# An MLP half rewritten: GELU in one ScalarE instruction, 64-row matmul pairs for a short K-chunk, bias taken off TensorE

## The chip, the cores and the metric

The kernel runs on one core of a Trainium2 chip. The metric is the device time of one execution, in microseconds (us). Engines are called PE (TensorE matmul), PEld (TensorE weight load, which overlaps PE), DVE (VectorE), ACT (ScalarE), POOL (GpSimd) and SP (SyncE, which only issues transfers here). The profile's span is a little shorter than the time (607.4 against 609.1 us for the kernel before). A ratio below is the mean time of one kernel's fast runs over that of the other's fast runs of the same rounds, so it is not quite the ratio of the medians that are quoted beside it.

## The reference

One transformer layer: layer norm, a linear-attention mixer, a residual add, two more layer norms, an MLP with GELU, and a second residual add. 2048 tokens, width 576, hidden width 4608, bf16. The change lies in the MLP:

```python
def _B_ref(x, w1, b1, w2, b2):
    y = _layernorm(x, axis=-1)
    h = _gelu(jnp.einsum("bsd,df->bsf", y, w1) + b1)     # tanh form
    return jnp.einsum("bsf,fd->bsd", h, w2) + b2

h  = x + _A_ref(_layernorm(x), ...)                      # attention part
h2 = h + _B_ref(_layernorm(h), B_w1, B_b1, B_w2, B_b2)   # MLP part
```

576 is not a multiple of 128: the contraction over it falls into four chunks of 128 rows and one of 64.

## The kernel before

The MLP works on blocks of 512 tokens (four in all). FF1 makes hidden features in m-tiles of 128 (36 of them), FF2 contracts them again. Before that a stage called LN2 here normalizes all 16 token tiles and transposes them into `ln2T`. The fifth K-chunk is padded with zero rows (cuts marked `# ...`):

```python
ln2T = []
for c in range(NKC):                       # KC = [128, 128, 128, 128, 64]
    t = persist.tile([P, S], BF16, ...)
    if KC[c] < P:
        nc.gpsimd.memset(t[:, :], 0.0)     # padding, done in the set-up
# ... attention part ...
w1c[4]: nc.gpsimd.memset(t, 0.0), then a DMA of 64 rows
w2t: first half on the SP queue, second half on the POOL queue
# LN2: per pair of token tiles: tensor_scalar on DVE, transposes (128 x 128, the last one
# 128 x 64), PSUM to SBUF on ACT (chunks 0, 2, 4) and DVE (chunks 1, 3)
for b in range(NBK):
    for half in range(2):                                    # 18 m-tiles each
        h1T = hpool.tile([P, NHALF, 512], BF16, ...)         # one buffer
        for pair in range(NHALF // 2):
            for i in range(2):                               # FF1: 5 matmuls of 128x512
                # ...
                nc.scalar.activation(x1[:, i, :], ph, AF.Identity, bias=b1col[:, m : m + 1])
            nc.vector.tensor_tensor(ga, x1, x1, ALU.mult)    # GELU by hand
            nc.vector.tensor_scalar(gb, ga, GELU_A, 1.0, ALU.mult, ALU.add)
            nc.vector.tensor_tensor(gc, gb, x1, ALU.mult)
            nc.scalar.activation(gs, gc, AF.Sigmoid, scale=GELU_C2)
            nc.vector.tensor_tensor(h1T[:, mm0 : mm0 + 2, :], x1, gs, ALU.mult)
        for j in range(4):                                   # FF2: 18 x (512 + 64 columns)
            if half == 0:                                    # b2 as two one-row matmuls
                nc.tensor.matmul(po1[:, 0:512], ones_row, b2row[:, 0:512], start=True, stop=False)
                nc.tensor.matmul(po2[:, 0:64], ones_row, b2row[:, 512:D], start=True, stop=False)
            # ... matmuls over mm, then h_all[:, t] += po1, po2 on DVE
    # ... ot = copy(h_all) on ACT, DMA out
```

The softmax here doesn't subtract the row's maximum and nothing guards it: scores larger than these inputs give would overflow.

## Time and profile before

The time is 609.06 us (median of 4 runs). The attention part ends at about 268 us; the MLP takes the rest.

| Part of the MLP, in a steady block of 512 tokens | us | Read from |
|---|---|---|
| FF1, 180 matmuls of 128x512, one every 0.216 us | 38.9 | timeline |
| FF2, 144 pairs of 512 + 64 columns, one every 0.245 us | 35.3 | timeline |
| b2, 4 pairs of one-row matmuls, 0.47 us each | 1.9 | timeline |
| rest: mostly PE waiting at FF1-to-FF2 borders | 3.4 | 79.53 minus the above |
| one block | 79.53 | first FF1 matmul of a block to that of the next |

These groups of instructions are from the page of the kernel before. The columns are: line, engine, operation, output from inputs and shapes, count; busy us and mean ns of one; idle us just before them and what ended most of it.

```profile
L579 PE MATMUL ph<-ln2T,w1c 128*128 128x512 bf16 x720 | 157.6, 380 | 0.0
L615 PE MATMUL po<-w2t,h1T 128*128 128x512 bf16 x576 | 146.8, 381 | 11.7 <-DVE h1T L598 11.4
L585 ACT ACTIVATE x<-ph,b1col 128x512 bf16<-128x512 f32 x144 | 91.9, 681 | 74.5 <-PE ph L579 74.5
L589 DVE TENSOR_TENSOR ga<-x 128x1024 bf16<-128x1024 bf16 x72 | 49.6, 689 | 22.3 <-ACT x L585 22.3
L597 ACT ACTIVATE gs<-gc 128x1024 bf16<-128x1024 bf16 x72 | 75.9, 1055 | 22.8 <-DVE gc L595 22.8
L598 DVE TENSOR_TENSOR h1T<-x,gs 128x1024 bf16<-128x1024 bf16 x72 | 49.5, 687 | 10.4 <-ACT gs L597 9.7
```

FF1 (L579) never waits. The first FF2 matmuls (L615) wait 11.4 us for `h1T`, the last step of the GELU chain. That chain costs DVE 0.69 + 0.43 + 0.69 + 0.69 = 2.5 us per pair of m-tiles, which overlap to 2.27 where DVE doesn't wait (timeline, 376.02 to 378.29 us) and to some 2.35 on average, while PE makes a pair in 10 x 0.216 = 2.16 us. So DVE falls behind through the half, and PE pays at the border. ACT has little slack either: where it doesn't wait, its two Identities and the Sigmoid take 2.09 us per pair (374.74 to 376.83).

The next lines are from the timeline around one pair of b2 matmuls: start and duration in us, then the instruction. The durations overlap (0.39 us for 512 columns that start every 0.216 us) and the ends are modelled, so starts are to be compared.

```profile
399.22 0.19 PE L621 MATMUL po<-w2t,h1T 128*128 128x64 bf16 x1
399.34 0.39 PE L606 MATMUL po<-b2row,ones_row 1*128 1x512 bf16 x1
399.57 0.19 PE L609 MATMUL po<-b2row,ones_row 1*128 1x64 bf16 x1
399.69 0.39 PE L615 MATMUL po<-w2t,h1T 128*128 128x512 bf16 x1
```

From 399.22 to 399.69 is 0.47 us, of which the ordinary 64-column matmul's own slot is 0.03. At each change between 128 rows and 1 row some 0.09 us is lost: 399.34 - 399.22 is 0.12 where an ordinary 64-column matmul takes 0.03.

### The profile page before, as it was taken

To read this page: it belongs to the slowest core of one execution; us is meant where nothing else is said; L and a number is where in the kernel's file an instruction comes from. 1 tells how busy PE (TensorE), PEld (TensorE's weight loads), DVE (VectorE), ACT (ScalarE), POOL (GpSimd) and SP (SyncE) were. 2 spreads that over 40 slices of the span, in tenths; PEclk is the share of its full clock that TensorE was granted. 3 is DMA by queue.
4 is the path that set the end of the run, shared out by engine and by line. 5 is a ranking of instruction groups with operands and counts; after the bars stand their busy time and mean duration, and the time that the engine had idled before them with its cause. 6 is when DMAs were issued, how large, how long until landed. Compare 5 with 4: busy or idle time off the path is not lost.

```text
span 607.4 us, 9204 instructions
## 1 busy us (share of the span) xinstructions
PE 506.7 (83%) x3626; PEld 268.9 (44%) x3626; DVE 396.6 (65%) x997; ACT 271.7 (45%) x470; POOL 35.5 (6%) x95
## 2 busy tenths in 40 slices
PE   0169777987878788759999999999899998999986
PEld 0136546773344544425444444444444444444443
DVE  3807998651588889985864928639468195492771
ACT  1155678525303030014944818429266084480661
POOL 8620000020000000030000000000000000000000
PEclk9999789797669697776999999999999999999999
DMA  8000000010000000049600000000000000000001
GB/s 288 2 0 3 1 0 2 2 29 16 1 2 1 1 1 1 2 165 326 210 2 1 0 30 11 0 1 1 21 19 1 1 1 11 30 0 2 1 1 39
DMA packets 10261, 18.61 MB, mean 31 GB/s; under 512 B 1513, under 2 KB 8490, under 8 KB 9642
## 3 DMA queue, kind: packets, MB, share of 16 engines
q1 hardware_dynamic: 9049, 15.36, 7.5%
q0 software_dynamic: 1168, 2.67, 1.4%
q8 instruction: 28, 0.46, 0.3%
q14 instruction: 16, 0.12, 0.1%
HBM read 15.66 MB, written 2.36 MB: 30 GB/s over the span
## 4 chain that ended last, share of the span: by engine, by line
DVE 44%; PE 41%; ACT 10%; issue 3%; DMA 2%; POOL 1%; ACTq 0%; DVEq 0%; POOLq 0%
PE po L615 15%; DVE h1T L598 7%; DVE gc L595 7%; PE ph L579 6%; DVE ga L589 6%; DVE gb L591 4%; ACT gs L597 3%; DVE sk L300 3%; DVE phik L309 3%; PE pbr L411 2%; ACT eq L386 2%; PE po L621 2%; PE pao L480 2%; PE pt L551 2%; PE pkA L285 2%
## 5 line engine op out<-in xcount | busy, mean ns | idle before, releaser
L579 PE MATMUL ph<-ln2T,w1c 128*128 128x512 bf16 x720 | 157.6, 380 | 0.0
L615 PE MATMUL po<-w2t,h1T 128*128 128x512 bf16 x576 | 146.8, 381 | 11.7 <-DVE h1T L598 11.4
L585 ACT ACTIVATE x<-ph,b1col 128x512 bf16<-128x512 f32 x144 | 91.9, 681 | 74.5 <-PE ph L579 74.5
L621 PE MATMUL po<-w2t,h1T 128*128 128x64 bf16 x576 | 109.5, 193 | 0.0
L579 PEld LDWEIGHTS <-w1c 128*128 128x128 bf16 x720 | 69.6, 98 | 84.5 <-DMA w1c<-in_B_w_dram 0.5
L615 PEld LDWEIGHTS <-h1T 128*128 128x128 bf16 x576 | 56.3, 98 | 84.1 <-DVE h1T L598 17.0
L597 ACT ACTIVATE gs<-gc 128x1024 bf16<-128x1024 bf16 x72 | 75.9, 1055 | 22.8 <-DVE gc L595 22.8
L627 DVE TENSOR_TENSOR h_all<-h_all,po 128x512 f32<-128x512 f32 x32 | 22.0, 689 | 89.2 <-PE po L621 89.2
L589 DVE TENSOR_TENSOR ga<-x 128x1024 bf16<-128x1024 bf16 x72 | 49.6, 689 | 22.3 <-ACT x L585 22.3
L621 PEld LDWEIGHTS <-h1T 128*128 128x128 bf16 x576 | 56.1, 98 | 1.5
L598 DVE TENSOR_TENSOR h1T<-x,gs 128x1024 bf16<-128x1024 bf16 x72 | 49.5, 687 | 10.4 <-ACT gs L597 9.7
L595 DVE TENSOR_TENSOR gc<-gb,x 128x1024 bf16<-128x1024 bf16 x72 | 49.6, 688 | 1.2
L386 ACT ACTIVATE eq<-ppq 128x512 bf16<-128x512 f32 x40 | 21.6, 595 | 60.4 <-PE ppq L377 60.4
L636 ACT CAST ot<-h_all 128x576 bf16<-128x576 f32 x16 | 10.7, 671 | 51.4 <-DVE h_all L630 51.4
L317 PE MATMUL pv<-wv,ln1T 128*128 128x504 bf16 x80 | 24.4, 423 | 10.7 <-DVE ln1T L275 6.6
L591 DVE TENSOR_SCALAR gb<-ga 128x1024 bf16<-128x1024 bf16 x72 | 30.8, 427 | 2.4
L402 DVE RECIPROCAL recrow<-psS 128x80 bf16<-128x80 f32 x16 | 10.5, 658 | 25.2 <-PE psS L394 25.0
L413 DVE TENSOR_TENSOR phiq<-eq,pbr 128x512 bf16<-128x512 bf16 x40 | 24.3, 681 | 3.0 <-PE pbr L411 3.0
L285 PEld LDWEIGHTS <-ln1T 128*128 128x128 bf16 x400 | 24.9, 104 | 0.8
L300 DVE TENSOR_REDUCE sk<-phik 128x64 f32<-128x1152 bf16 x16 | 21.2, 1331 | 5.9 <-ACT phik L296 5.8
L377 PE MATMUL ppq<-ln1T,Wq 128*128 128x512 bf16 x100 | 24.8, 410 | 0.0
L285 PE MATMUL pkA<-Wk,ln1T 128*128 128x128 bf16 x320 | 23.7, 232 | 0.0
(129 smaller groups left out, 592.8 us busy)
## 6 DMA issues: line engine op xcount, KB each, us to landing
w1c<-in_B_w_dram SPq DMA_DIRECT2D x4, 1152.0 KB
w2t<-in_B_w_dram POOLq DMA_DIRECT2D x1, 2592.0 KB, 23.1
w2t<-in_B_w_dram SPq DMA_DIRECT2D x1, 2592.0 KB
x_all<-in_A_x_dram SPq DMA_DIRECT2D x1, 2304.0 KB
out_dram<-ot SPq DMA_DIRECT2D x16, 144.0 KB
wqkv<-in_A_wqkv_dram SPq DMA_DIRECT2D x4, 432.0 KB
w1c<-in_B_w_dram SPq DMA_DIRECT2D x1, 576.0 KB
wog<-in_A_wo_dram SPq DMA_DIRECT2D x4, 141.8 KB
```

What stands on the lines that cost most here:

```text
L285: nc.tensor.matmul(dst, ln1T[c][:, t * 128 : (t + 1) * 128], wkp[(g, c)][:, :], start=(c == 0), stop=(c == NKC - 1),)
L300: nc.vector.tensor_reduce(sk[:, :], phik[:, t, :, :].rearrange("p s (h f) -> p (s h) f", f=DH), AX.X, ALU.add,)
L386: nc.scalar.activation(eq[:, :], ppq[:, :], AF.Exp, scale=sc)
L579: nc.tensor.matmul(ph[:, :], w1c[c][:, m * 128 : (m + 1) * 128], ln2T[c][:, b * 512 : (b + 1) * 512], start=(c == 0), stop=(c == NKC - 1),)
L585: nc.scalar.activation(x1[:, i, :], ph[:, :], AF.Identity, bias=b1col[:, m : m + 1], scale=1.0)
L589: nc.vector.tensor_tensor(ga[:, :, :], x1[:, :, :], x1[:, :, :], ALU.mult)
L591: nc.vector.tensor_scalar(gb[:, :, :], ga[:, :, :], GELU_A, 1.0, ALU.mult, ALU.add)
L595: nc.vector.tensor_tensor(gc[:, :, :], gb[:, :, :], x1[:, :, :], ALU.mult)
L597: nc.scalar.activation(gs[:, :, :], gc[:, :, :], AF.Sigmoid, scale=GELU_C2)
L598: nc.vector.tensor_tensor(h1T[:, mm0 : mm0 + 2, :], x1[:, :, :], gs[:, :, :], ALU.mult)
L615: nc.tensor.matmul(po1[:, 0:512], h1T[:, mm, j * 128 : (j + 1) * 128], w2t[:, m, 0:512], start=st_, stop=(mm == NHALF - 1),)
L621: nc.tensor.matmul(po2[:, 0 : D - 512], h1T[:, mm, j * 128 : (j + 1) * 128], w2t[:, m, 512:D], start=st_, stop=(mm == NHALF - 1),)
```

## The change

Its intent is to make PE the only limit of the MLP and to give it less to do. (1) GELU becomes one ACT instruction per m-tile. (2) b2 is broadcast once by DMA; POOL adds it to the residual ahead of time, and one DVE instruction makes the output tile. (3) The 64-row chunk is not padded: the weights of m-tile i sit on partitions 0 to 63, those of m-tile i+18 on 64 to 127, `ln2T[4]` holds its 64 rows twice, and the two 64-row matmuls stand side by side. They come last for even i and first for odd i, so two pairs meet. (4) FF1 runs over all 36 m-tiles before FF2; FF2 splits its columns 288 + 288. (5) All weights go through the SP queue; the paddings' memsets go. (6) PSUM: four banks for FF1 and LN2, two double-bank tiles for FF2.

```diff
-        if KC[c] < P:
-            nc.gpsimd.memset(t[:, :], 0.0)                   # ln2T padding
...
+        w1e = dpool.tile([P, NM // 2, P], BF16, name="w1e", tag="w1e")
+        for o in range(2):
+            nc.sync.dma_start(w1e[64 * o : 64 * o + 64, :, :], B_w1[512:D, o * FF // 2 : ...])
...
+                    nc.scalar.copy(ln2j[:, D : D + 64], ln2j[:, 512:D])   # rows twice
...
+                def rest(first):
+                    for o in range(2):
+                        r = slice(64 * o, 64 * o + 64)
+                        nc.tensor.matmul(phs[o], w1e[r, i, :], ln2T[4][r, tok], start=first, stop=not first)
+                odd = i % 2 == 1
+                if odd: rest(True)
+                for o in range(2): ...                       # 4 full matmuls each
+                if not odd: rest(False)
-                    ga, gb, gc, gs ... (DVE, DVE, DVE, ACT), h1T (DVE)
+                    nc.scalar.activation(h1T[:, m, :], phs[o], AF.Gelu_apprx_tanh, bias=b1col[:, m : m + 1])
...
-                        nc.tensor.matmul(po1[:, 0:512], ones_row[:, :], b2row[:, 0:512], ...)
-                        nc.tensor.matmul(po2[:, 0 : D - 512], ones_row[:, :], b2row[:, 512:D], ...)
+                nc.gpsimd.tensor_tensor(hb[:, :], h_all[:, t, :], b2bc[:, :], ALU.add)
+                nc.vector.tensor_tensor(ot, hb, pot[:, :, 0:288], ALU.add)
```

More of the change, by code (lines that the diff above doesn't have):

```diff
@@ L67 @@
     persist = ctx.enter_context(tc.tile_pool(name="persist", bufs=1))
-    psum = ctx.enter_context(tc.tile_pool(name="psum", bufs=6, space=bass.MemoryType.PSUM))
-    psum2 = ctx.enter_context(tc.tile_pool(name="psum2", bufs=1, space=bass.MemoryType.PSUM))
     actx = ctx.enter_context(ExitStack())
+    psum = actx.enter_context(tc.tile_pool(name="psum", bufs=6, space=bass.MemoryType.PSUM))
+    psum2 = actx.enter_context(tc.tile_pool(name="psum2", bufs=1, space=bass.MemoryType.PSUM))
     apool = actx.enter_context(tc.tile_pool(name="apool", bufs=1))
@@ L113 @@
     make_identity(nc, ident)
-    ones_row = consts.tile([1, P], BF16, name="ones_row", tag="ones_row")
-    nc.vector.memset(ones_row[:], 1.0)
     eps_ap = consts.tile([P, 1], FP32, name="eps_ap", tag="eps_ap")
     nc.vector.memset(eps_ap[:], EPS)
-    b2row = consts.tile([1, D], BF16, name="b2row", tag="b2row")
-    nc.sync.dma_start(b2row[:, :], B_b2.rearrange("(o f) -> o f", o=1))
+    b2bc = consts.tile([P, D], BF16, name="b2bc", tag="b2bc")
+    nc.sync.dma_start(b2bc[:, :], B_b2.rearrange("(o f) -> o f", o=1).to_broadcast([P, D]))
     b1nat = consts.tile([FF // P, P], BF16, name="b1nat", tag="b1nat")
@@ L520, with ln2_stage @@
         dpool = dctx.enter_context(tc.tile_pool(name="dpool", bufs=1))
+        pf = dctx.enter_context(tc.tile_pool(name="pf", bufs=4, space=bass.MemoryType.PSUM))
+        po = dctx.enter_context(tc.tile_pool(name="po", bufs=2, space=bass.MemoryType.PSUM))
+        NM = FF // P
         w1c = []
-        for c in range(NKC):
+        for c in range(4):
             t = dpool.tile([P, FF], BF16, name=f"w1c{c}", tag=f"w1c{c}")
-            if KC[c] < P:
-                nc.gpsimd.memset(t[:, :], 0.0)
-            nc.sync.dma_start(t[: KC[c], :], B_w1[KOFF[c] : KOFF[c] + KC[c], :])
+            nc.sync.dma_start(t[:, :], B_w1[KOFF[c] : KOFF[c] + P, :])
             w1c.append(t)
-        w2t = dpool.tile([P, FF // P, D], BF16, name="w2t", tag="w2t")
+        w1e = dpool.tile([P, NM // 2, P], BF16, name="w1e", tag="w1e")
+        for o in range(2):
+            nc.sync.dma_start(
+                w1e[64 * o : 64 * o + 64, :, :],
+                B_w1[512:D, o * FF // 2 : (o + 1) * FF // 2].rearrange("k (i p) -> k i p", p=P),
+            )
+        w2t = dpool.tile([P, NM, D], BF16, name="w2t", tag="w2t")
         w2v = B_w2.rearrange("(m p) f -> p m f", p=P)
         nc.sync.dma_start(w2t[:, 0:18, :], w2v[:, 0:18, :])
-        nc.gpsimd.dma_start(w2t[:, 18:36, :], w2v[:, 18:36, :])
+        nc.sync.dma_start(w2t[:, 18:36, :], w2v[:, 18:36, :])
         lnp2 = dctx.enter_context(tc.tile_pool(name="lnp2", bufs=4))
         small2 = dctx.enter_context(tc.tile_pool(name="small2", bufs=1))
+        hpool = dctx.enter_context(tc.tile_pool(name="hpool", bufs=1))
+        outp = dctx.enter_context(tc.tile_pool(name="outp", bufs=3))
+        hbp = dctx.enter_context(tc.tile_pool(name="hbp", bufs=2))
         rst2_all = small2.tile([P, NT], FP32, name="rst2_all", tag="rst2_all")
         nc.scalar.sqrt(rst2_all[:, :], ln2_r2[:, :])
-        for b in range(NBK):
+        def ln2_stage(b):
             for jp in range(2):
@@ L541 @@
                     t = 4 * b + j
-                    ln2j = lnp2.tile([P, D], BF16, name="ln2", tag="ln2")
+                    ln2j = lnp2.tile([P, D + 64], BF16, name="ln2", tag="ln2")
                     nc.vector.tensor_scalar(
-                        ln2j[:, :], h_all[:, t, :], ln2_mean[:, t : t + 1], rst2_all[:, t : t + 1],
+                        ln2j[:, 0:D], h_all[:, t, :], ln2_mean[:, t : t + 1], rst2_all[:, t : t + 1],
                         ALU.subtract, ALU.mult,
                     )
+                    nc.scalar.copy(ln2j[:, D : D + 64], ln2j[:, 512:D])
@@ L547 @@
                     ln2.append(ln2j)
+                tbase = (4 * b + 2 * jp) * 128
                 for c in range(NKC):
-                    pt = psum.tile([P, 256], BF16, name="pt2", tag="p1")
+                    pt = pf.tile([P, 256], BF16, name="pt2", tag="pf")
                     for jj in range(2):
                         nc.tensor.transpose(
-                            pt[: KC[c], jj * 128 : (jj + 1) * 128],
-                            ln2[jj][:, KOFF[c] : KOFF[c] + KC[c]],
-                            ident[:, :],
+                            pt[:, jj * 128 : (jj + 1) * 128], ln2[jj][:, c * P : (c + 1) * P], ident[:, :]
@@ L555 @@
                         )
-                    tbase = (4 * b + 2 * jp) * 128
                     if c % 2 == 0:
-                        nc.scalar.copy(ln2T[c][: KC[c], tbase : tbase + 256], pt[: KC[c], :])
+                        nc.scalar.copy(ln2T[c][:, tbase : tbase + 256], pt[:, :])
                     else:
-                        nc.vector.tensor_copy(ln2T[c][: KC[c], tbase : tbase + 256], pt[: KC[c], :])
-        hpool = dctx.enter_context(tc.tile_pool(name="hpool", bufs=1))
-        x1p = dctx.enter_context(tc.tile_pool(name="x1p", bufs=3))
@@ L566 @@
-        gpool = dctx.enter_context(tc.tile_pool(name="gpool", bufs=2))
-        outp = dctx.enter_context(tc.tile_pool(name="outp", bufs=2))
-        for b in range(NBK):
-            for half in range(2):
-                h1T = hpool.tile([P, NHALF, 512], BF16, name="h1T", tag="h1T")
-                for pair in range(NHALF // 2):
-                    mm0 = pair * 2
-                    x1 = x1p.tile([P, 2, 512], BF16, name="x1", tag="x1")
-                    for i in range(2):
-                        m = half * NHALF + mm0 + i
-                        ph = psum.tile([P, 512], FP32, name="ph", tag="p1")
-                        for c in range(NKC):
-                            nc.tensor.matmul(
-                                ph[:, :],
-                                w1c[c][:, m * 128 : (m + 1) * 128],
-                                ln2T[c][:, b * 512 : (b + 1) * 512],
-                                start=(c == 0), stop=(c == NKC - 1),
-                            )
-                        nc.scalar.activation(
-                            x1[:, i, :], ph[:, :], AF.Identity, bias=b1col[:, m : m + 1], scale=1.0
-                        )
-                    ga = gpool.tile([P, 2, 512], BF16, name="ga", tag="gab")
-                    nc.vector.tensor_tensor(ga[:, :, :], x1[:, :, :], x1[:, :, :], ALU.mult)
-                    gb = gpool.tile([P, 2, 512], BF16, name="gb", tag="gab")
-                    nc.vector.tensor_scalar(
-                        gb[:, :, :], ga[:, :, :], GELU_A, 1.0, ALU.mult, ALU.add
-                    )
-                    gc = gpool.tile([P, 2, 512], BF16, name="gc", tag="gc")
-                    nc.vector.tensor_tensor(gc[:, :, :], gb[:, :, :], x1[:, :, :], ALU.mult)
-                    gs = gpool.tile([P, 2, 512], BF16, name="gs", tag="gs")
-                    nc.scalar.activation(gs[:, :, :], gc[:, :, :], AF.Sigmoid, scale=GELU_C2)
-                    nc.vector.tensor_tensor(
-                        h1T[:, mm0 : mm0 + 2, :], x1[:, :, :], gs[:, :, :], ALU.mult
-                    )
-                for j in range(4):
-                    t = 4 * b + j
-                    po1 = psum.tile([P, 512], FP32, name="po1", tag="p1")
-                    po2 = psum.tile([P, 136], FP32, name="po2", tag="p1")
-                    if half == 0:
-                        nc.tensor.matmul(
-                            po1[:, 0:512], ones_row[:, :], b2row[:, 0:512], start=True, stop=False
-                        )
-                        nc.tensor.matmul(
-                            po2[:, 0 : D - 512], ones_row[:, :], b2row[:, 512:D], start=True, stop=False
-                        )
-                    for mm in range(NHALF):
-                        m = half * NHALF + mm
-                        st_ = (mm == 0) and (half == 1)
-                        nc.tensor.matmul(
-                            po1[:, 0:512],
-                            h1T[:, mm, j * 128 : (j + 1) * 128],
-                            w2t[:, m, 0:512],
-                            start=st_, stop=(mm == NHALF - 1),
-                        )
-                        nc.tensor.matmul(
-                            po2[:, 0 : D - 512],
-                            h1T[:, mm, j * 128 : (j + 1) * 128],
-                            w2t[:, m, 512:D],
-                            start=st_, stop=(mm == NHALF - 1),
-                        )
-                    nc.vector.tensor_tensor(
-                        h_all[:, t, 0:512], h_all[:, t, 0:512], po1[:, 0:512], ALU.add
-                    )
-                    nc.vector.tensor_tensor(
-                        h_all[:, t, 512:D], h_all[:, t, 512:D], po2[:, 0 : D - 512], ALU.add
-                    )
@@ new lines, in ln2_stage, with ff1_stage @@
+                        nc.vector.tensor_copy(ln2T[c][:, tbase : tbase + 256], pt[:, :])
+        def ff1_stage(b):
+            h1T = hpool.tile([P, NM, 512], BF16, name="h1T", tag="h1T")
+            tok = slice(b * 512, (b + 1) * 512)
+            for i in range(NM // 2):
+                phs = [pf.tile([P, 512], FP32, name="ph", tag="pf") for o in range(2)]
+                def rest(first):
+                    for o in range(2):
+                        r = slice(64 * o, 64 * o + 64)
+                        nc.tensor.matmul(
+                            phs[o][:, :], w1e[r, i, :], ln2T[4][r, tok], start=first, stop=not first,
+                        )
+                odd = i % 2 == 1
+                if odd:
+                    rest(True)
+                for o in range(2):
+                    m = i + NM // 2 * o
+                    for c in range(4):
+                        nc.tensor.matmul(
+                            phs[o][:, :], w1c[c][:, m * 128 : (m + 1) * 128], ln2T[c][:, tok],
+                            start=(c == 0 and not odd), stop=(c == 3 and odd),
+                        )
+                if not odd:
+                    rest(False)
+                for o in range(2):
+                    m = i + NM // 2 * o
+                    nc.scalar.activation(
+                        h1T[:, m, :], phs[o][:, :], AF.Gelu_apprx_tanh,
+                        bias=b1col[:, m : m + 1], scale=1.0,
+                    )
+            return h1T
@@ L633, with ff2_stage @@
+        def ff2_stage(b, h1T):
             for j in range(4):
                 t = 4 * b + j
-                ot = outp.tile([P, D], BF16, name="ot", tag="ot")
-                nc.scalar.copy(ot[:, :], h_all[:, t, :])
-                nc.sync.dma_start(out_ptd[:, t, :], ot[:, :])
+                pot = po.tile([P, 2, 512], FP32, name="pot2", tag="po")
+                for m in range(NM):
+                    for s in range(2):
+                        nc.tensor.matmul(
+                            pot[:, s, 0:288],
+                            h1T[:, m, j * 128 : (j + 1) * 128],
+                            w2t[:, m, 288 * s : 288 * s + 288],
+                            start=(m == 0), stop=(m == NM - 1),
+                        )
+                ot = outp.tile([P, 2, 288], BF16, name="ot", tag="ot")
+                hb = hbp.tile([P, D], FP32, name="hb", tag="hb")
+                nc.gpsimd.tensor_tensor(hb[:, :], h_all[:, t, :], b2bc[:, :], ALU.add)
+                nc.vector.tensor_tensor(
+                    ot[:, :, :], hb[:, :].rearrange("p (s d) -> p s d", s=2),
+                    pot[:, :, 0:288], ALU.add,
+                )
+                nc.sync.dma_start(out_ptd[:, t, :], ot[:, :, :].rearrange("p s d -> p (s d)"))
@@ L641 @@
+        for b in range(NBK):
+            ln2_stage(b)
+        for b in range(NBK):
+            ff2_stage(b, ff1_stage(b))
 _INS = ['A_x', 'A_wqkv', 'A_w_phi', 'A_wo', 'B_x', 'B_w1', 'B_b1', 'B_w2', 'B_b2']
```

## The prediction

> **What bounds the kernel now.** The attention part is untouched by the change except for set-up; it lasts until about 268 us (timeline). The MLP part runs from 284 us (first steady FF1 matmul, timeline) to 602.5 us, 318 us of the 607.4 us span. In its windows PE is 96% busy at a granted clock of 1.00, so PE is the limit, with gaps. Per block of 512 tokens, from the timeline:
> - FF1: 180 matmuls 128x512, started every 0.216 us: 38.9 us (155.5 us for four blocks).
> - FF2: 144 pairs (512 + 64 columns), one pair every 0.245 us: 35.3 us (141 us).
> - b2 row matmuls: a pair takes 0.47 us from the end of the previous stream to the next one (two one-row matmuls plus about 0.09 us at each change of row count): 16 pairs, 7.5 us.
> - The rest, about 14 us, is the GELU tail at each FF1-to-FF2 border: the wait view gives PE 11.4 us on DVE h1T. The chain of waits runs there through gc, gs and h1T, because DVE needs 2.4 us per pair of m-tiles (0.69+0.43+0.69+0.69) against PE's 2.16.
>
> **What the change does.**
> 1. GELU becomes one ACT instruction per m-tile. Identity from PSUM takes 0.68 us here, and the Trainium skill ("ScalarE: Activation LUTs", step-by-step) says that every function has the same rate per element. So 1.36 us per pair against PE's ~2.0: ACT keeps up, DVE falls nearly idle, the borders close because the last m-tiles are needed about 4 us into FF2. Gain 13 us.
> 2. b2 leaves PE for POOL and the final add, ahead of time. Gain 7.5 us.
> 3. The zero-padded fifth K-chunk becomes two 64-row matmuls on both halves of the array. The Trainium skill ("TensorE: Matmul & The Clock Gate", Part 3) says that such row groups run concurrently; no run here shows it yet. If so, 72 slots of 0.216 us go: 15.5 us. Against this stand 72 mode changes (the skill, "TensorEngine Tiling", Key Properties, says a change drains the array); at the 0.09 to 0.1 us read around the b2 matmuls that is 7 us. Net 8 us.
> 4. FF2 as 288+288 columns: the same 576 columns per weight tile, the pair stays near 0.245 us. No gain, no loss.
> 5. LN2 stage: DVE sets its pace now (1.06+0.51 = 1.57 us per two tiles, no gap). DVE's work stays; ACT gets two small copies (0.93 to about 1.4 us, an estimate from its copies); the 0.2 us breaks around 64-column transposes vanish. Unchanged within 1 us.
> 6. All weights on one queue, w1 first, without the 3.9 us memset before its last chunk: w1 no longer shares bandwidth with half of w2. FF1 waited 0.5 us for it: at most 1 us.
> 7. Tail: the ACT cast (0.67 us plus hand-over) goes: 0.9 us.
>
> **Sum.** 13+7.5+8+1+0.9 = 30 us, all on PE's path. New MLP: 147+141+1 = 289 us from 284 us, then 4 us of tail: span 578, time **580 us**, range **573 to 591**. Chances: faster by over 2% 0.95, within 2% 0.04, slower 0.01.
>
> **What would show it.** PE above 98% busy after 290 us; no PE wait on h1T; DVE below 10% there, ACT near 65% in FF1 only; the two 64-row matmuls starting within some 10 ns of each other; FF1 about 36.8 us and FF2 35.3 us per block; about 0.1 us lost at each mode change.
>
> **What would make it wrong.** Row groups that run one after the other: 16 us back, about 596. Mode changes costing 0.2 us: 7 us more. 288-column matmuls exposing weight loads (0.098 us each). The clock falling under denser work. A scheduler order that lets FF1 wait for LN2's PSUM buffers, now four.

## The result, and the profile after

The changed kernel takes 575.62 us (median of 8 runs, 573.9 to 576.99) against 609.01 (13 runs). The ratio is 0.9448, with a 95% interval of 0.9435 to 0.946.

The groups of the changed kernel that answer to those of before (same columns):

```profile
L594 ACT ACTIVATE h1T<-ph,b1col 128x512 bf16<-128x512 f32 x144 | 92.1, 685 | 161.8 <-PE ph L576 155.7
L606 PE MATMUL pot<-w2t,h1T 128*128 128x288 bf16 x1152 | 141.8, 286 | 0.0
L586 PE MATMUL ph<-ln2T,w1c 128*128 128x512 bf16 x576 | 132.4, 382 | 0.0
L615 DVE TENSOR_TENSOR ot<-hb,pot 128x576 bf16<-128x576 f32 x16 | 12.1, 754 | 279.1 <-PE pot L606 279.1
```

No PE group of FF1 or FF2 waits any more. GELU costs 685 ns, Identity before cost 681. The four instructions of the DVE chain are gone; DVE's only work in the MLP after LN2 is the last line.

One period of FF1 in the timeline of the changed kernel (four m-tiles):

```profile
361.80 0.61 PE L576 MATMUL ph<-ln2T,w1e 64*128 64x512 bf16 x4
362.34 3.63 PE L586 MATMUL ph<-ln2T,w1c 128*128 128x512 bf16 x16
365.90 0.39 PE L576 MATMUL ph<-ln2T,w1e 64*128 64x512 bf16 x2
```

The period is 365.90 - 361.80 = 4.10 us. The four 64-row matmuls hold PE for 362.34 - 361.80 = 0.54 us, with the change back to 128 rows, not for 4 x 0.216 = 0.86. The chain of waits after 320 us is one unbroken run of PE work:

```profile
351.95 1.73 PE ph L586 x8
354.21 3.56 PE ph L586 x16
...
386.99 1.83 PE ph L586 x8
388.82 35.28 PE pot L606 x288
424.10 1.73 PE ph L586 x8
```

FF1 takes 388.82 - 351.95 = 36.87 us, FF2 35.28, a block 72.15 us instead of 79.53. In the windows view PE is busy for 45.00 of 45 us from 330 us on, at a granted clock of 1.00:

```profile
330.00:375.00 45.00, 45.00 (x294) 26.39 (x292) 2.26 (x3) 13.26 (x21) 3.82 (x3) 1.00 0.03 11
```

(Columns: window, its length, then busy us of PE, PEld, DVE, ACT and POOL with counts, the clock, the DMA share and GB/s.) DVE has 2.26 us of work in 45.

### The profile page after: what moved, and what is told of

Same layout as the page of the kernel before. It is cut to its first block, busy times and chain, and to the rows that moved or that the text cites. A ratio compares the mean times of both kernels' runs of the same rounds, so it can differ in the third digit from the quotient of the medians.

```text
span 572.3 us, 8653 instructions
## 1 busy us (share of the span) xinstructions
PE 483.6 (85%) x3594; PEld 293.5 (51%) x3594; DVE 214.3 (37%) x660; ACT 197.2 (34%) x398; POOL 49.1 (9%) x108
## 4 chain that ended last, share of the span: by engine, by line
PE 67%; DVE 21%; ACT 6%; issue 2%; DMA 2%; POOL 1%; POOLq 0%; ACTq 0%; DVEq 0%
PE pot L606 25%; PE ph L586 23%; PE ph L576 3%; DVE sk L295 3%; DVE phik L304 3%; PE pbr L406 3%; ACT eq L381 3%; DMA wqkv<-in_A_wqkv_dram 2%; DVE recrow L397 2%; PE pkA L280 2%; PE pao L475 2%; DVE otok L435 1%; PE pv L312 1%; PE pW L212 1%; DVE phiq L408 1%
## 5 line engine op out<-in xcount | busy, mean ns | idle before, releaser
L594 ACT ACTIVATE h1T<-ph,b1col 128x512 bf16<-128x512 f32 x144 | 92.1, 685 | 161.8 <-PE ph L576 155.7
L606 PE MATMUL pot<-w2t,h1T 128*128 128x288 bf16 x1152 | 141.8, 286 | 0.0
L586 PE MATMUL ph<-ln2T,w1c 128*128 128x512 bf16 x576 | 132.4, 382 | 0.0
L586 PEld LDWEIGHTS <-w1c 128*128 128x128 bf16 x576 | 53.5, 98 | 74.9 <-issue 17.0
L614 POOL TENSOR_TENSOR hb<-h_all,b2bc 128x576 f32<-128x576 f32 x16 | 20.4, 1274 | 401.2 <-DVE ot L615 349.9
L576 PE MATMUL ph<-ln2T,w1e 64*128 64x512 bf16 x144 | 22.4, 381 | 0.0
L475 PE MATMUL pao<-wog,oT 128*128 128x512 bf16 x80 | 21.6, 403 | 0.6 <-DVE oT L468 0.6
L287 ACT ACTIVATE phik<-pkA 128x504 bf16<-128x504 f32 x32 | 19.4, 615 | 6.5 <-PE pkA L280 6.4
L304 DVE TENSOR_TENSOR phik<-phik,rk 128x1152 bf16<-128x1152 bf16 x16 | 21.1, 1334 | 0.0
L406 PE MATMUL pbr<-recT,LT 80*128 80x512 bf16 x40 | 17.7, 626 | 1.2 <-DVE recT L400 1.2
```

The lines of the kernel that those rows point to most:

```text
L304: nc.vector.tensor_tensor(phik[:, t, :, :].rearrange("p s (h f) -> p s h f", f=DH), phik[:, t, :, :].rearrange("p s (h f) -> p s h f", f=D ...
L406: nc.tensor.matmul(pbr[:, :], LT[idx][0:80, :], recT[0:80, :], start=True, stop=True)
L475: nc.tensor.matmul(pao1[:, 0:512], oTs[j][:, g, :], wog[g][:, 0:512], start=(g == 0), stop=(g == NG - 1),)
L576: nc.tensor.matmul(phs[o][:, :], w1e[r, i, :], ln2T[4][r, tok], start=first, stop=not first,)
L586: nc.tensor.matmul(phs[o][:, :], w1c[c][:, m * 128 : (m + 1) * 128], ln2T[c][:, tok], start=(c == 0 and not odd), stop=(c == 3 and odd),)
L594: nc.scalar.activation(h1T[:, m, :], phs[o][:, :], AF.Gelu_apprx_tanh, bias=b1col[:, m : m + 1], scale=1.0,)
```

## The experiments

All outputs are right. Names with b_ start from the kernel before, those with a_ from the changed kernel. "Steady block" is the distance of the first FF1 matmuls of two successive blocks in the trace; it is far less noisy than whole times.

### b_gelu: the GELU alone

```diff
-   x1 = Identity(ph) on ACT; ga, gb, gc on DVE; gs = Sigmoid on ACT; h1T on DVE
+   nc.scalar.activation(h1T[:, mm0 + i, :], ph[:, :], AF.Gelu_apprx_tanh, bias=b1col[:, m : m + 1])
```

> The kernel before with only the GELU moved to one ACT instruction per m-tile (still two half passes, zero-padded fifth chunk, b2 on PE). Theory (the border gaps are the DVE chain's tail): the waits of PE on h1T, 11.4 us before, vanish, 13 to 14 us less, about 595.5 us. Rival (the gaps come from the border itself, whichever engine does the GELU, or from the buffers): under 5 us less.

Measured: 593.84 us, ratio 0.9747 (0.9734 to 0.9759), that is 15.4 us. No wait of PE on `h1T` is left:

```profile
L584 ACT ACTIVATE h1T<-ph,b1col 128x512 bf16<-128x512 f32 x144 | 98.2, 687 | 131.4 <-PE ph L578 131.3
L601 PE MATMUL po<-w2t,h1T 128*128 128x512 bf16 x576 | 144.0, 381 | 0.0
```

The steady block falls from 79.53 to 75.94 us, 14.4 us over four blocks. The theory holds, the rival (borders cost by themselves) falls: there are still eight borders here, and none waits. This one edit is nearly half of the whole gain. It takes the chain off DVE and the Sigmoid off ACT at once, so it shows that the chain caused the waits; that DVE set its pace is read from the trace of before.

### b_b2: b2 alone

```diff
-   16 pairs of one-row matmuls
+   for j in range(4): nc.gpsimd.tensor_tensor(h_all[:, t, :], h_all[:, t, :], b2bc[:, :], ALU.add)
```

> The kernel before with only b2 taken off PE: POOL adds it into the residual ahead of time, the one-row matmuls go. Theory: each pair cost 0.47 us on PE, 16 pairs, 7.5 us less, about 601.5 us. Rival (at a border PE waits for h1T anyway, so the eight row pairs that stand first after a border, half of the blocks' sixteen or fewer, hid in that wait): 5 to 6 us less. A second rival: the POOL adds slow DVE's chain in the first block, which would eat 1 us or more.

Measured: 611.17 us, ratio 1.0034 (1.0015 to 1.0053): slower, by 0.3%. The first rival is right, and the second in part: POOL slowed DVE, but in LN2 and not in the GELU chain. First, the steady block falls only from 79.53 to 78.15 us: 1.39 us, three pairs of 0.46 rather than four. The wait of PE on `h1T` grows from 11.4 to 12.7 us; a pair that stood first after a border had filled time in which PE waited anyway. That gives 5.5 us. Second, LN2 lost more than that. These are timeline lines of LN2, first of the kernel before, then of b_b2 (DVE and POOL):

```profile
275.03 0.50 DVE L560 COPY ln2T<-pt 128x256 bf16<-128x256 bf16 x2
275.45 1.06 DVE L543 TENSOR_SCALAR ln<-h_all,ln_mean,rst_all 128x576 bf16<-128x576 f32 x2
276.60 0.50 DVE L560 COPY ln2T<-pt 128x256 bf16<-128x256 bf16 x2
```

```profile
269.01 22.87 POOL L570 TENSOR_TENSOR h_all<-h_all,b2bc 128x576 f32<-128x576 f32 x16
276.80 2.58 DVE L541 TENSOR_SCALAR ln<-h_all,ln_mean,rst_all 128x576 bf16<-128x576 f32 x2
279.30 0.48 DVE L558 COPY ln2T<-pt 128x256 bf16<-128x256 bf16 x2
279.69 2.58 DVE L541 TENSOR_SCALAR ln<-h_all,ln_mean,rst_all 128x576 bf16<-128x576 f32 x2
```

The scheduler placed all POOL adds beside LN2. While they run, two normalizations take DVE 2.58 us instead of 1.06, whereas the copies from PSUM keep their 0.5. The Trainium skill ("GPSIMD Engine Reference", section 1, Specifications) says that POOL's SBUF interfaces are shared with VectorE, with contention for DVE instructions in a 2-port mode or with two SBUF inputs; the traces agree in that the instruction that reads SBUF suffers and the one that reads PSUM doesn't. Whether the normalization runs in such a mode the traces don't show. The first FF1 matmul starts 22.9 us after LN2's table load (266.03 to 288.90) instead of 14.3 (268.17 to 282.46), 8.6 us more. The changed kernel escapes this: with two buffers for `hb` POOL runs only two adds ahead, at 182 us, long before LN2; the others wait for DVE's output adds.

### b_gelu_b2: both

```diff
    (on top of b_gelu; nothing on POOL)
-   nc.scalar.copy(ot[:, :], h_all[:, t, :])
+   nc.vector.tensor_tensor(ot[:, :], h_all[:, t, :], b2bc[:, :], ALU.add)
```

> As b_gelu, and b2 off PE as well, this time added by DVE in the place of the last ACT cast, so that nothing collides with LN2. Measured so far: b_gelu 593.8 us; in b_b2 the steady block got only 1.39 us shorter, three row pairs of 0.46 us, the fourth having stood at a border where PE waited for h1T anyway. Theory (without the border wait all four pairs of a block count): 1.9 us per block, 7.5 us less than b_gelu, 586.3 us. Rival (only three in four ever count): 5.5 us less, 588.3 us.

Measured: 587.01 us, ratio 0.9614 (0.9598 to 0.9631), 1.3% or 8 us below b_gelu. The steady block is 74.13 us, 1.81 below b_gelu's 75.94, or 7.2 us over four. With no wait at the borders all four pairs count: the theory holds.

### a_serial: the 64-row pair on the same rows

```diff
-   r = slice(64 * o, 64 * o + 64);   w1e[r, i, :]
+   r = slice(0, 64);                 w1e[r, i + NM // 2 * o, :]
```

> The changed kernel with both 64-row matmuls of a pair on rows 0 to 63 (the second no longer on rows 64 to 127), nothing else but one output buffer less. Theory (the gain of the row pairs is that they run at the same time): 72 slots of 0.216 us come back, 15.5 us, about 591 us; the two of a pair start 0.216 us apart instead of a few ns. Rival (the gain is from elsewhere, K=64 matmuls being cheaper by themselves): under 5 us more.

Measured: 591.64 us, ratio 0.9675 (0.9657 to 0.9693). FF1 takes 40.74 us per block instead of 36.87, 15.5 us over four blocks, against 72 x 0.216 = 15.55 us for the slots. The four matmuls now take 363.39 - 362.42 = 0.97 us instead of 0.54 (timeline of a_serial):

```profile
362.42 1.03 PE L572 MATMUL ph<-ln2T,w1e 64*128 64x512 bf16 x4
363.39 3.63 PE L582 MATMUL ph<-ln2T,w1c 128*128 128x512 bf16 x16
```

So the gain is that the two row halves run at the same time, as the Trainium skill ("TensorE: Matmul & The Clock Gate", Part 3) has it. In the changed kernel the two matmuls of a pair start 3 to 4 ns apart in 70 of the 72 pairs. The other two pairs in time, both in the first block, start 226 ns apart, with four full matmuls between these pairs: there the order on PE is another one.

### a_pad: the padded chunk again

```diff
-   two 64-row matmuls per pair of m-tiles
+   nc.gpsimd.memset(w1e[64:P, :], 0.0); five full matmuls per m-tile
```

> The changed kernel with the zero-padded fifth chunk of before: five full matmuls per m-tile, no 64-row matmuls, no mode changes. Theory: FF1 goes back from 36.9 to 38.9 us per block, 8 us more in all, about 583.7 us. Rival (mode changes cost as much as the row pairs save): 0 to 2 us more.

Measured: 584.48 us, ratio 0.957 (0.9546 to 0.9594). The steady block is 74.13 us, 1.98 more than the changed kernel's 72.15, or 7.9 us over four. It equals that of b_gelu_b2: apart from the row pairs, GELU and b2 nothing of the change moves a steady block. (a_serial and a_pad also have one output buffer less; FF2 takes 35.28 us per block in both, as in the changed kernel.)

### a_nogroup: every pair of 64-row matmuls last

```diff
-   odd = i % 2 == 1
+   odd = False
```

> The changed kernel with the 64-row pair always last, never two pairs side by side: 144 mode changes instead of 72. Theory (one change costs about 0.11 us on PE, read from 0.54 us for two pairs of 0.216 us): 8 us more, about 583.5 us, so as slow as the padded one. Rival (the drain is hidden, the grouping is for the PSUM buffers only): under 2 us.

Measured: 583.54 us, ratio 0.9547 (0.9524 to 0.9571). FF1 takes 38.78 us per block, 1.91 more, with 18 more mode changes per block: 1.91 / 18 = 0.106 us for one change. The timeline shows it, a pair now costing 363.23 - 362.91 = 0.32 us where the stream itself needs 0.216:

```profile
362.91 0.39 PE L576 MATMUL ph<-ln2T,w1e 64*128 64x512 bf16 x2
363.23 1.90 PE L586 MATMUL ph<-ln2T,w1c 128*128 128x512 bf16 x8
```

The Trainium skill ("TensorEngine Tiling (Array Packing)", Key Properties) says that a change of tiling mode drains the engine; it gives no time. Without grouping, the row pairs save nothing over zero padding: 38.78 us against 38.85 in a_pad. The gain hangs on letting two pairs meet.

### a_512: FF2 split as before

```diff
-   288 + 288 columns, one final add
+   512 + 64 columns, two final adds
```

> The changed kernel with FF2 split 512 + 64 columns as before, and two final adds. Theory (streamed columns set the pace, 0.245 us per pair either way): within 1 us of 575.6. Rival (equal halves hide the weight loads better): 3 us more or above, FF2 over 36 us per block.

Measured: 575.09 us, ratio 0.9412 (0.9387 to 0.9437), not told from the changed kernel (0.9448, 0.9435 to 0.946; the intervals touch). FF2 takes 35.27 us per block against 35.28. The split has no effect on PE.

### b_ln2 and b_ln2_nomemset: LN2 alone, with and without the set-up memset

```diff
+   nc.scalar.copy(ln2j[:, D : D + 64], ln2j[:, 512:D])     # all transposes 128 wide
    (b_ln2_nomemset also:)
-   nc.gpsimd.memset(ln2T[4], 0.0)
```

> The kernel before with only the LN2 stage of the changed kernel: a copied 64-column tail so that all transposes are 128 wide, set-up memset kept. Theory (the 64-column transposes cost about 0.2 us of PE pause each way and these paced the stage at 1.575 us per two tiles): about 2 us less, 607 us, the stage's period falling to about 1.47 us. Rival, as the prediction had it (DVE paces the stage at 1.57 us): 0 to 0.5 us less, period unchanged.

> As b_ln2, and the 1.81 us POOL memset of the padded tile left out (the copied tail fills it). The order on PE, DVE, ACT and SP is the same in both; only POOL's differs. Theory (POOL's chain of mask building paces the set-up, so the memset delays all that follows): 1.5 us less than b_ln2, seen already at the first projection matmul. Rival A (the attention part's 4 us came from it wholly, through clock phases): 3 to 4 us less. Rival B (no effect; the 4 us were the luck of one profile): 0.

Measured: b_ln2 608.25 us, ratio 0.9989 (0.9968 to 1.001), no gain clear of noise. LN2's period went from 1.575 to 1.55 us only (starts of successive pairs of normalizations), so my theory of the 64-column pauses falls. What LN2 did save was met in part by the wait of PE for w1, 0.5 us in the kernel before and now 1.0 (line of the wait view: us in total, times, longest):

```profile
PEld L580 <- DMA w1c<-in_B_w_dram: 1.0, 1, 1.0
```

In the changed kernel, where w1 goes ahead of all of w2 on one queue and needs no memset, no such wait shows. Its LN2 period was 1.46 us. What differs is the granted clock (windows view of b_ln2, of the changed kernel and of a_pad, columns as above):

```profile
270.00:276.00 6.00, 5.46 (x43) 3.87 (x41) 5.78 (x18) 5.06 (x21) 0.00 (x0) 0.50 1.01 412
270.00:276.00 6.00, 4.10 (x43) 2.74 (x41) 6.00 (x18) 5.39 (x21) 0.00 (x0) 1.00 1.02 385
270.00:276.00 6.00, 5.13 (x38) 3.74 (x37) 5.63 (x15) 4.76 (x19) 0.00 (x0) 0.50 1.05 416
```

At 1.00 the transposes start 0.055 us apart, and DVE is busy for 6.00 of 6 us; at 0.50, as in the kernel before too, they start 0.107 us apart. a_pad and a_serial have the changed kernel's LN2 code, but got 0.50 there, and their period was 1.67. In a_ref it went from 1.46 to 1.73 after the clock fell (0.50 from 277 to 279 us). So 1.57, which the prediction read as DVE's pace, was not DVE's limit. The shorter LN2 came with the clock: at 0.50 the changed code, at 1.67, is slower than that of before. Why the full clock was granted in some executions only is not shown.

b_ln2_nomemset: 606.66 us, ratio 0.9954 (0.9938 to 0.9971), 0.35% or 2.1 us below b_ln2, the intervals just overlapping. The memset stands in the middle of POOL's mask building (timeline of the kernel before, POOL):

```profile
27.90 1.79 POOL L234 MEMSET ln2T<- 128x2048 bf16 x1
29.65 0.28 POOL L159 TENSOR_SCALAR_AFFINE_SELECT rr<-ra 8x128 bf16<-8x128 bf16 x1
29.90 0.24 POOL L188 TENSOR_SCALAR_AFFINE_SELECT sel<-rzer 8x80 bf16<-8x80 bf16 x1
```

### a_ref and a_memset: the changed kernel again, and with that memset put back

```diff
    (a_memset)
+   nc.gpsimd.memset(ln2T[4], 0.0)
```

> The changed kernel again, for comparison on this chip: 575.6 us, ratio 0.945. If the attention part's 4 us were the luck of one profile, its profile may show the LN2 stage starting at 266 us or later instead of 264.2.

> The changed kernel with the 1.81 us POOL memset of before put back into the set-up (its result is overwritten later). Order on all other engines unchanged. Theory (POOL paces the set-up): 1.5 us more than a_ref. Rival: 0, or all of the 4 us.

Measured: a_ref 577.25 us, ratio 0.9443 (0.9419 to 0.9466); a_memset 578.48 us, ratio 0.9472 (0.9454 to 0.949). The memset costs 0.3%, 1.8 us by the means, with an uncertainty as large. The traces support its sign: the first weight-folding transposes on PE start at 35.1 to 35.4 us in the six profiles with the memset, and at 33.7 to 34.6 in the eight without. LN2's table load starts at 267.2 us on average in the six and at 266.3 in the eight, but single ones differ by over 3 us. About 1 us is what the traces show; whether it is 1 or 2 us at the end these runs don't settle.

a_ref also explains a false lead. In the first profile after the change, LN2's table load started at 264.18 us, 4 us before that of the kernel before (268.17), though the order of instructions on PE, DVE and ACT is the same up to there. In a_ref, the same program, it started at 267.56. So most of those 4 us were a difference between two executions. The granted clock in the attention part differed too: 0.87 against 0.83 from 100 to 150 us. The Trainium skill ("TensorE: Matmul & The Clock Gate", Part 1) says that the window by which the clock is granted runs free and that the effect varies from run to run. The traces agree in that the clocks differ; that this is the whole cause is argued, not shown.

### best: LN2 of later blocks inside the first FF1

```diff
-   for b in range(NBK): ln2_stage(b)                       # all LN2 before all FF1
+   ln2_pair(0, 0), ln2_pair(0, 1)                           # block 0 only
+   in ff1_stage(0), at i = 3, 5, ..., 13: ln2_pair of blocks 1 to 3,
+       transposes into FF2's idle PSUM tiles, evicted by DVE, tail copy on POOL
+   w1 loaded in two groups of columns (m-tiles 0-4 of each half first)
```

> The changed kernel with w1 loaded in two groups of columns (m-tiles 0 to 4 of each half first) and LN2 of blocks 1 to 3 put between the FF1 matmuls of block 0, its evictions on DVE, the tail copies on POOL. Theory (before the first FF1 matmul PE idles in LN2 for some 12 us, of which only the first block's 3 us are needed): FF1 starts near 270 us instead of 278, 3.5 us of transposes go back into FF1: 4 to 5 us less, about 571 us. Rival (w1 arrives too late, or the transposes break up FF1 and cost mode changes): no gain.

Measured: 572.69 us (571.95 to 574.38), ratio 0.9388 (0.9368 to 0.9409), against a_ref's 0.9443 in the same rounds: 0.55% or 3.4 us faster, a little less than the 4 to 5 us expected. The first FF1 matmul of best:

```profile
271.49 1.06 PE L596 MATMUL ph<-ln2T,w1c 128*128 128x512 bf16 x2
```

That is 5.5 us after its table load (266.01), where a_ref needs 14.4 (267.56 to 281.97); some 5 us of this go back into a longer first FF1, since FF2 of the first block starts 49.2 us after the table load (315.25) instead of 52.9 (320.41 in a_ref). It is the fastest version found, ahead of both kernels.

## Why the prediction was right or wrong

It was right: 575.6 us lies in 573 to 591, "faster by over 2%" came true, and the mechanism holds in the three terms that carry the gain. Of the small ones, term 5 (LN2) has the right size for a partly wrong reason, and term 6 (w1) was not tested. The point, 580, was 4.4 us too high. The steady blocks can be accounted for nearly exactly:

| Term | predicted, us | measured over four blocks, us | from |
|---|---|---|---|
| GELU on ACT, borders closed | 13 | 14.4 | b_gelu, 79.53 to 75.94 per block |
| b2 off PE | 7.5 | 7.2 | b_gelu_b2, 75.94 to 74.13 |
| 64-row pairs, net of mode changes | 8 | 7.9 | a_pad, 74.13 to 72.15 |
| sum | 28.5 | 29.5 | 79.53 to 72.15 |

1. GELU. "Gain 13 us" was a little low; its mechanism, a slow GELU chain that PE pays for at the border, is shown by b_gelu. The Trainium skill ("ScalarE: Activation LUTs", step-by-step) says that all functions have one rate; here GELU took 685 ns and Identity 681. ACT was to be near 65% busy in FF1: 22.26 of 35.10 us, 63%.
2. b2. "Gain 7.5 us" is right only beside the GELU edit. Alone it was 5.5 us in the blocks, because a quarter of the pairs stood in time that PE waited away. Terms of such a sum depend on what else is taken away.
3. Row pairs. 15.5 us of slots back (a_serial: 15.5) against 72 mode changes of 0.106 us, 7.6 us (predicted 7). The 0.09 us read around the old one-row matmuls came close, though it was lucky that changes to 64 rows cost much the same as those to one row, which no run had shown.
4. "The pair stays near 0.245 us": a_512 shows it.
5. "LN2 unchanged within 1 us". From the table load to the first FF1 matmul of block 1 takes 95.5 us before and 88.2 in a_ref; less one steady block each, that is 16.0 in both (15.5 in the first profile after). So the term is right for the time, but partly by luck. LN2's last copy ends 16.4 us after the table load before and 15.0 in a_ref (14.5 in the first profile after), with the clock as told under b_ln2. Yet FF1 starts no earlier: its first matmul comes after 14.3 us before and 14.4 in a_ref (13.8), because before it two FF1 matmuls ran ahead of LN2's last five transposes. The first block is then longer than a steady one by 1.7 us before and 1.6 in both profiles after. In the first of these some 1.0 us of it is the clock (the first five matmuls start up to 0.43 us apart) and 0.6 the two split groups of 64-row matmuls told under a_serial.
6. "At most 1 us" for w1 on one queue: not tested alone; b_ln2 shows that the wait for w1 is next in line when LN2 gets shorter.
7. Tail: from the start of DVE's adds for the last tile to the end 4.7 us before and 3.8 after: 0.9, as predicted.

The step that was missing is the set-up. The prediction took the attention part as "untouched by the change except for set-up" and gave the set-up no time. The memset that was dropped there was worth some 1 to 2 us, with an uncertainty as large; that POOL paces the set-up fits the traces, but is not shown beyond that. Together: 29.5 + 0.9 + 1 to 2 = 31.4 to 32.4 of the 33.4 us between the medians. The remaining 1 to 2 us is not assigned. The attention part could hold it: its end, LN2's table load, lies between 264.2 and 267.6 us in the eight profiles without the memset.

## What to carry to other kernels

Read the steady period of each stage from starts in the trace and add up its terms: here that gave the change's worth to within 1 us in 29, where whole times scatter by as much as the smaller terms. Packing two short-K matmuls into the halves of the array pays only if the mode changes cost less than the slots saved: here two changes of 0.106 us ate up one slot of 0.216, so place the pairs so that they meet. Before work is moved to an idle engine, ask when it will run and what runs beside it: the same POOL adds cost nothing to be seen behind two buffers and some 9 us beside a DVE stage. And compare the granted clock of a stage before explaining its pace by its code.

## What the Trainium skill lacked or had wrong

- "TensorEngine Tiling (Array Packing)", Key Properties, says that a mode change drains the engine and gives no time. Here it cost 0.106 us of PE for 128 to 64 rows or back, between 512-column matmuls (a_nogroup), and about 0.09 us around the one-row matmuls of before.
- "TensorE: Matmul & The Clock Gate", "Back-to-back issue gap", gives about 131 ns per matmul as the sustained figure for 512 columns in a stream of weight loads and matmuls. In this case such a stream ran at 216 ns, which is what the same section calls the isolated gap (512 / 2.4 + 2.5); 288 columns took 122.5 ns.
- "GPSIMD Engine Reference", section 1, Specifications, names the contention with VectorE but no size. Two 128x576 fp32-to-bf16 normalizations on DVE took 2.58 us beside fp32 adds on POOL, and 1.06 without; the adds started 1.45 us apart and the period of LN2 was 2.90, two adds. The skill treats this contention more fully elsewhere; only the size for this case is new.
